# Sigmoid attention and SwiGLU in one launch: the order written out from changed planner constants, and another way of storing the last set

## The chip, the cores and the metric

The kernel runs on one core of a Trainium2 chip. The time is the device time of one execution in microseconds (us). Of the kernel before there are three timed runs, with a median of 419.71 us (419.66 to 421.11), and one profiled execution, from which every duration below is taken.

## The reference

Two blocks follow one another. The first is attention with a sigmoid in place of the softmax, on inputs of 8 batches, 12 heads, 448 rows and 64 columns:

```python
scores = scale * np.matmul(q, k.transpose(0, 1, 3, 2)) - np.log(S)
attn = 1.0 / (1.0 + np.exp(-scores))
attn_out = np.matmul(attn, v)
```

Its output, with the heads laid side by side, is x, of 3584 rows and 768 columns. The second block is a feed-forward layer of width 1536:

```python
g = x @ w_gate
silu = g * (1.0 / (1.0 + np.exp(-g)))
return (silu * (x @ w_val)) @ w_out
```

All inputs and the output are float32 in device memory.

## The kernel before

**The blocks of attention.** Four heads of a batch make a block, so a batch has 3 blocks and the whole 24, numbered i = 0 to 23. For a block the kernel loads q, k and v (448 KB each) to staging buffers, casts q and k to bf16 and v to fp16, and transposes q and k. For blocks 0 to 5 TensorE transposes (`tr_pe`, L337: seven 128x128 transposes for q and seven for k, each set copied from PSUM to the tile `qkT` by VectorE). For later blocks one transposing DMA on SyncE does both (`tr_dma`, L370). A block has 7 key slots. For each there is a burst of four score matmuls (`burst`, L381, tile `sc`) and one sigmoid on ScalarE (`sig`, L405: `pt`, 128x896, the longest kind of instruction of ScalarE here). Then 28 matmuls multiply by v (`pv`, L413), and two copies give `xT`, the transposed x that the second block reads.

**The feed-forward block.** `f1` (L455) takes a batch and one of 12 slices of 128 of the 1536 columns: six matmuls give `g`, six give `v`; ScalarE takes the sigmoid of `g` (`s`), VectorE multiplies it by `g` (`t`, which frees the PSUM slot of `g`) and then by `v` (`hT`). The tiles `g` and `v` share a ring of two PSUM slots, so the `g` of a slice waits until `t` of the slice before has read its own `g`. The gate and value weights come in four chunks (`wg_0` to `wv_3`), each loaded in three parts of 384 KB and cast by GpSimd. The last product, with w_out, is done for two blocks of 128 rows at a time (`f2_set`, L549) in a form with seven products of six matmuls instead of eight, numbered 1 to 7, whose results VectorE adds up in the output tile; sums of the weights for it are formed by VectorE (`weight_sums`, L512).

**What sets the order.** Each instruction or small group is first recorded as an operation with an engine, an assumed duration, what it depends on and which buffers it takes and gives back. A planner (`list_schedule`, L63) plays these through with its own account of time and writes all engines' instructions out in the order in which they would start; on the chip only semaphores hold. The account of a load is the line L40: one busy time per DMA from the number and size of its pieces, all loads in one chain. Two loads are lengthened by hand in the lines before `fill` (L691): the second part of k of block 0, and q of block 1. `MARGIN` (L59) is a time by which the planner lets a TensorE transpose of a block above 3 (blocks 4 and 5, L361) wait beyond the end of its cast. In the first stage, until the first `pv` of block 1, the planner also writes filler matmuls (`ps_warm`) where TensorE would idle. None of these figures is an instruction; they act through the order alone.

**The queues.** All loads, the transposing DMAs and the last stores are issued by SyncE in order. Casts of loads run on GpSimd in order, those of blocks 0 to 2 for q and k on VectorE.

**The end.** The last set (products 1 to 7 for m = 3, k = 3; tags `A` and `TO` are two PSUM rings) is stored in halves of 384 columns as soon as a half is complete (`store`, L608). A block of 128 rows there consists of two lots of 64 rows that lie at different places in the output. Before, the first lot goes out on SyncE's queue and the second on ScalarE's. The order is: half `lo` of e after `c11`, half `hi` of o after `c22`, half `hi` of e after `c12`, and half `lo` of o after `c21`, the add behind product 4 (`step7`, L668), the last of all.

Of the kernel before, what the change touches and what calls it, by code (L numbers as in the profile page):

```python
# [9 lines left out]
FP32 = mybir.dt.float32  # L10
# [17 lines left out]
class Op:  # L28
# [3 lines left out]
    def __init__(self, eng, dur, fn, deps=(), mode=("F", "F"), take=(), give=(), desc=(0, 0)):  # L32
        self.eng, self.dur, self.fn, self.mode = eng, dur, fn, mode
        self.deps = [d if isinstance(d, tuple) else (d, 0.0) for d in deps if d is not None]
        self.take = [Slot(t) for t in take]
        self.give = list(give)
        self.rank = self.t0 = self.t1 = None
        n, size = desc
        self.hold = n == 1792
        self.dma = 2.0 if n == 1792 else n / 16 * max(0.042, 0.003 + size / 24600)  # L40

    def got(self, tag):
        return [s for s in self.take if s.tag == tag]
# [12 lines left out]
NEAR = 12  # L56
VIS = 9
WO = 4
MARGIN = 0.0  # L59
FREE = set()  # L60


# [90 lines left out]
def kernel(  # L153
# [10 lines left out]
    nc = tc.nc  # L164

    B, H, S, D = q.shape
    DM = H * D
    DFF = moe_w_gate.shape[1]
    KC = DM // 128
    NF = DFF // 128  # L170
    NS = 7
# [35 lines left out]
    NH = NF // 2  # L207
# [5 lines left out]
    def wsum(j, c, n=1):  # L213

        x = (j - 1) * NH + c
        o = x % 4 * HW
        return stt[NEARLY + x // 4].bitcast(FP16)[:, o:o + n * HW]
# [6 lines left out]
    def op(*a, **kw):  # L224
        o = Op(*a, **kw)
        ops.append(o)
        return o
# [10 lines left out]
    T = {}  # L238
# [310 lines left out]
    def f2_set(m, k):  # L549


        last = k == NS // 2
        e, o = ((m - 1, NS - 1), (m, NS - 1)) if last else ((m, 2 * k), (m, 2 * k + 1))
        end = last and m == B // 2 - 1
        lo, hi = slice(0, HW), slice(HW, DM)
        P, C = {}, {}

        def blk(t, r):
            if t[0] != m:
                return kept[:, 3 * r:3 * r + 3]  # L560
            x = T["hT", m][:, r * NH:(r + 1) * NH, t[1] * 128:(t[1] + 1) * 128]
            return x.rearrange("p (a b) t -> p a b t", b=2)

        def hs(f0, f1):
            bs = {x // S for tm, t in (e, o) for x in (t * 128, t * 128 + 127) if tm == m}
            return [(R["hT", 2 * m + b, f], 0.16 * (f - f0)) for b in bs for f in range(f0, f1)] + \
                ([R["kept", m - 1, r] for r in range(2)] if last else [])

        def c(t, cols):
            return T[("osb",) + t][:, cols]  # L570

        def start(final):
            full = [d[0] if isinstance(d, tuple) else d for d in hs(0, NF)]

            def s1():
                for n in (1, 2):
                    T["s", n, m, k] = sb.tile([128, NH // 2, 2, 128], FP16, tag=f"S{n}", bufs=slots["S"],
                                              name=f"s{n}_{m}_{k}")
                nc.vector.tensor_tensor(out=T["s", 1, m, k], in0=blk(o, 0), in1=blk(o, 1), op=ADD)

            def s2():
                nc.vector.tensor_tensor(out=T["s", 2, m, k], in0=T["s", 1, m, k], in1=blk(e, 0), op=SUB)

            def s3():
                nc.vector.tensor_tensor(out=blk(o, 0), in0=blk(e, 0), in1=blk(o, 0), op=SUB)  # L585
            C["s1"] = op("DVE", 0.56, s1, deps=full, take=["S"])
            C["s2"] = op("DVE", 0.56, s2, deps=[C["s1"]])
            C["s3"] = op("DVE", 0.56, s3, deps=[C["s2"]])

        def product(n, lhs, rhs, deps, final):  # L590
            tag = "A" if final and n % 2 else "TO"

            def fn():
                if tag == "A":
                    T["p", m, k, n] = psum.tile([128, 2, 512], FP32, tag="A", bufs=2, name="ps_ol")[:, 0, 0:HW]
                else:
                    T["p", m, k, n] = psum.tile([128, HW], FP32, tag="TO", bufs=2, name="ps_o")
                for x in range(NH):
                    nc.tensor.matmul(out=T["p", m, k, n], lhsT=lhs()[:, x // 2, x % 2], rhs=rhs(x),  # L599
                                     start=x == 0, stop=x == NH - 1)  # L600
            P[n] = op("PE", 0.975, fn, deps=deps, take=[tag])

        def add(name, n, dst, other, deps, free=True):
            C[name] = op("DVE", 0.45, lambda: nc.vector.scalar_tensor_tensor(  # L604
                out=c(*dst), in0=T["p", m, k, n], scalar=HREC, in1=c(*other), op0=MULT, op1=ADD),
                deps=[P[n]] + deps, give=P[n].take if free else [])

        def store(t, deps, give, final, cols=slice(0, DM)):  # L608
            def fn(xs, dma):
                def go():  # L610
                    for x in xs:
                        bb, s = divmod(2 * t[1] + x, NS)
                        rows = slice((2 * t[0] + bb) * S, (2 * t[0] + bb + 1) * S)
                        dma.dma_start(out=out[rows, cols].rearrange("(p s) d -> s p d", s=NS)[s],  # L614
                                      in_=T[("osb",) + t][64 * x:64 * x + 64, cols])
                return go
            if end:
                op("SP", 0.5, fn([0], nc.sync), deps=deps, give=give)
                op("ACT", 0.5, fn([1], nc.scalar), deps=deps)
            else:  # L620
                op("SP" if final else "POOL", 1.1, fn([0, 1], nc.sync if final else nc.gpsimd), deps=deps, give=give)

        def step1(final):
            start(final)
            product(1, lambda: blk(e, 0), lambda x: wo16[:, x, lo],
                    hs(0, NH) + [R["wo16", f] for f in range(NF)], final)

            def fn():
                for t in (e, o):
                    if final:  # L630
                        T[("osb",) + t] = staging("osf")[:, 0:DM]
                    else:
                        T[("osb",) + t] = sb.tile([128, DM], FP32, tag="osb", bufs=slots["osb"],
                                                  name=f"osb_{t[0]}_{t[1]}")
                nc.scalar.activation(out=c(e, lo), in_=T["p", m, k, 1], func=COPY, scale=HREC)
            C["p1"] = op("ACT", 0.45, fn, deps=[P[1]], take=["osf" if final else "osb"] * 2, give=P[1].take)

        def step2(final):
            w = [R["ws", 4, x] for x in range(0, NH, 2)]
            product(6, lambda: T["s", 2, m, k], lambda x: wsum(2, x), [C["s2"]] + w, final)  # L640
            add("u2", 6, (e, hi), (e, lo), [C["p1"]])

        def step3(final):
            product(2, lambda: blk(e, 1), lambda x: wo16[:, NH + x, lo], hs(NH, NF), final)
            C["s4"] = op("DVE", 0.56, lambda: nc.vector.tensor_tensor(
                out=blk(e, 1), in0=blk(e, 1), in1=T["s", 2, m, k], op=SUB), deps=[P[2], C["s2"]])
            add("c11", 2, (e, lo), (e, lo), [C["u2"]])
            if end:
                store(e, [C["c11"]], [], final, lo)

        def step4(final):
            product(7, lambda: blk(o, 0), lambda x: wsum(3, x), [C["s3"]], final)
            add("u3", 7, (o, lo), (e, hi), [C["u2"]])

        def step5(final):
            product(5, lambda: T["s", 1, m, k], lambda x: wsum(1, x), [C["s1"]], final)
            add("u4", 5, (e, hi), (e, hi), [C["u3"]], free=False)
            add("c22", 5, (o, hi), (o, lo), [C["u3"]])
            P[5].give = C["s1"].take
            if end:  # L660
                store(o, [C["c22"]], [], final, hi)

        def step6(final):
            product(3, lambda: blk(e, 1), lambda x: wo16[:, NH + x, hi], [C["s4"]], final)
            add("c12", 3, (e, hi), (e, hi), [C["u4"]])
            store(e, [C["c11"], C["c12"]], C["p1"].take[:1], final, hi if end else slice(0, DM))

        def step7(final):  # L668
            product(4, lambda: blk(o, 1), lambda x: wsum(4, x), hs(NH, NF), final)
            add("c21", 4, (o, lo), (o, lo), [C["u3"], C["c22"]])  # L670
            store(o, [C["c21"], C["c22"]], C["p1"].take[1:], final, lo if end else slice(0, DM))
            R.setdefault(("f2", m), []).extend(P.values())
        return [(0.5, x) for x in (step1, step2, step3, step4, step5, step6, step7)]


# [10 lines left out]
    op("ACT", 1.5, lambda: nc.scalar.activation(out=warm, in_=sb_t, func=SIGM))  # L686
    loads(1, "qk")
    R["st_k", 0][1].dma += 1.0
    R["st_q", 1][0].dma += 0.4
    loads(0, "v")  # L690
    def fill(n):  # L691

# [151 lines left out]
```

## Time and profile before

| What | us |
|---|---|
| median of three runs | 419.71 |
| profiled execution: its own time | 420.82 |
| profiled execution: span from first to last instruction | 419.03 |
| TensorE busy | 410.4 (98%) |
| VectorE, ScalarE, GpSimd busy | 237.7, 217.5, 133.3 |
| mean granted TensorE clock | 0.999 of full |

In the profile PE is TensorE, PEld its weight loads, DVE VectorE, ACT ScalarE, POOL GpSimd and SP SyncE; a q behind a name is an engine's DMA-issuing sequencer. A timeline row gives the start in us, the busy time, the engine and the line, output tile and input, the number of merged instructions, and in brackets how long the engine had been idle before and what released it. A matmul's end is modelled and overlaps with the next one, so distances between starts are the better measure on PE. "To landing" is the time from the issue of a DMA to its completion. The time of an execution lies between 0.7 (the median) and 1.8 us (its own time) above the span; the span is what is worked with below.

### The profile page before, as it was taken

The page shows a single profiled execution, that of the slowest core. Times are in us where ns is not written, and L with a number is a line of the kernel's source. Part 1 is how long each engine was busy: PE and PEld are TensorE (multiplying, and loading weights), DVE is VectorE, ACT ScalarE, POOL GpSimd, SP SyncE. Part 2 cuts the span into 40 slices and gives each one's busy share as a digit, 9 for nine tenths or more (in the row PEclk, how much of TensorE's full clock was granted, in tenths as well). Part 3 has the DMA queues.
Part 4 walks back from the last instruction along what each step waited for, and adds up shares of the span by engine and source line. Part 5 has one row for each costly group of instructions (what it writes and reads, how often), then busy time and mean ns, then how long its engine had stood idle before and what let it go on. Part 6 is the DMA issues. An engine that isn't in the chain of part 4 may idle for free.

```text
span 419.0 us, 7945 instructions
## 1 busy us (share of the span) xinstructions
PE 410.4 (98%) x3194; PEld 205.1 (49%) x3194; DVE 237.7 (57%) x420; ACT 217.5 (52%) x290; POOL 133.3 (32%) x196
## 2 busy tenths in 40 slices
PE   8989999999999999999999999999999999999995
PEld 3434444444445554544454554554545545555563
DVE  3544544467667644564574745647556465565873
ACT  5986778778751165467445565455455552122000
POOL 1788865764360232424031431403400100000000
PEclk9999999999999999999999999999999999999999
DMA  8999999997980284488067373482500302020235
GB/s 266 380 375 377 375 286 340 314 314 184 229 248 2 76 215 83 150 172 236 2 177 125 127 223 74 140 144 100 120 2 0 77 2 75 2 74 1 60 95 150
DMA packets 64693, 66.97 MB, mean 160 GB/s; under 512 B 35536, under 2 KB 60880, under 8 KB 64656
## 3 DMA queue, kind: packets, MB, share of 16 engines
q1 hardware_dynamic: 62704, 59.39, 49.7%
q0 software_dynamic: 1632, 6.69, 6.3%
q8 instruction: 25, 0.41, 0.4%
q10 hardware_dynamic: 320, 0.39, 0.3%
q14 instruction: 12, 0.10, 0.1%
HBM read 47.19 MB, written 11.01 MB: 139 GB/s over the span
## 4 chain that ended last, share of the span: by engine, by line
PE 90%; DMA 6%; DVE 1%; ACT 1%; SPq 0%; issue 0%; POOL 0%; POOLq 0%
PE ps_g L466 26%; PE ps_v L466 23%; PE ps_o L599 18%; PE ps_sc L391 8%; PE ps_pv L426 7%; PE ps_ol L599 5%; DMA st<-in_k_dram 4%; PE ps_vl L466 3%; DMA st<-in_v_dram 3%; ACT pt L408 0%; SPq L265 0%; PE ps_tr L348 0%; DVE t L476 0%; DVE hT L585 0%; POOL src L235 0%
## 5 line engine op out<-in xcount | busy, mean ns | idle before, releaser
L408 ACT ACTIVATE pt<-ps_sc,sbiast 128x896 f16<-128x896 f32 x168 | 159.0, 1007 | 28.8 <-PE ps_sc L391 28.8
L466 PE MATMUL ps_g<-xT,wg 128*128 128x448 f16 x576 | 124.0, 353 | 0.5 <-DVE t L476 0.5
L472 ACT ACTIVATE s<-ps_g 128x448 f16<-128x448 f32 x96 | 52.2, 544 | 123.5 <-PE ps_g L466 122.7
L476 DVE TENSOR_TENSOR t<-ps_g,s 128x448 f16<-128x448 f32 x96 | 59.9, 624 | 92.3 <-ACT s L472 92.2
L466 PE MATMUL ps_v<-xT,wv 128*128 128x448 f16 x504 | 109.9, 353 | 0.0
L466 PEld LDWEIGHTS <-wg 128*128 128x128 f16 x576 | 54.9, 98 | 54.8 <-issue 6.7
L466 PEld LDWEIGHTS <-wv 128*128 128x128 f16 x576 | 52.0, 98 | 59.1 <-issue 17.6
L235 POOL CAST src<-st 128x896 bf16<-128x896 f32 (+1 forms) x43 | 40.3, 937 | 96.8 <-DMA st<-in_q_dram 66.7
L482 DVE SCALAR_TENSOR_TENSOR hT<-ps_v,t 128x448 f16<-128x448 f32 x84 | 52.4, 624 | 32.0 <-PE ps_v L466 31.1
L391 PE MATMUL ps_sc<-qkT 64*64 64x448 bf16 x672 | 50.8, 360 | 0.8 <-ACT pt L408 0.6
L599 PEld LDWEIGHTS <-hT 128*128 128x128 f16 x384 | 37.6, 98 | 27.2
L235 POOL CAST v<-st 64x448 f16<-64x448 f32 (+1 forms) x72 | 42.2, 586 | 22.4 <-DMA st<-in_v_dram 8.7
L614 POOL DMA_DIRECT2D out_dram<-osb x34 | 17.7, 525 | 93.6 <-DVE osb L604 93.5
L426 PE MATMUL ps_pv<-pt,v 64*64 64x448 f16 x672 | 37.7, 351 | 0.2
L604 DVE SCALAR_TENSOR_TENSOR osb<-ps_o,osb 128x384 f32<-128x384 f32 x63 | 34.0, 551 | 6.2 <-PE ps_o L599 6.2
L233 DVE CAST xT<-ps_pv 128x448 f16<-128x448 f32 x40 | 23.4, 619 | 20.7 <-PE ps_pv L426 20.7
L599 PE MATMUL ps_o<-wo,hT 128*128 128x384 f16 x168 | 31.9, 326 | 0.0
L391 PEld LDWEIGHTS <-qkT 64*64 64x64 bf16 x672 | 14.8, 105 | 29.0 <-issue 25.2
L426 PEld LDWEIGHTS <-v 64*64 64x64 f16 x672 | 19.3, 107 | 14.6 <-issue 3.8
L599 PE MATMUL ps_o<-st,s 128*128 128x384 f16 x138 | 26.2, 326 | 0.0
L599 PE MATMUL ps_o<-st,hT 128*128 128x384 f16 x138 | 26.2, 326 | 0.0
L599 PEld LDWEIGHTS <-s 128*128 128x128 f16 x168 | 16.4, 98 | 11.8
(44 smaller groups left out, 195.6 us busy)
## 6 DMA issues: line engine op xcount, KB each, us to landing
st<-in_q_dram SPq DMA_DIRECT2D x24, 448.0 KB, 5.3
st<-in_v_dram SPq DMA_DIRECT2D x24, 448.0 KB, 6.3
st<-in_k_dram SPq DMA_DIRECT2D x23, 448.0 KB, 5.5
out_dram<-osb POOLq DMA_DIRECT2D x34, 192.0 KB, 3.1
st<-in_moe_w_gate_dram SPq DMA_DIRECT2D x12, 384.0 KB, 8.8
st<-in_moe_w_val_dram SPq DMA_DIRECT2D x12, 384.0 KB, 8.8
st<-in_moe_w_out_dram SPq DMA_DIRECT2D x12, 384.0 KB, 6.9
out_dram<-st SPq DMA_DIRECT2D x16, 192.0 KB, 2.7
```

The source lines that it names most:

```text
L233: nc.vector.tensor_copy(out=o, in_=i)
L235: nc.gpsimd.tensor_copy(out=o, in_=i)
L391: nc.tensor.matmul(out=sc[64 * (g ^ a):64 * (g ^ a) + 64, a, 0:S].rearrange("k (s p) -> k s p", s=NS), lhsT=kT[r, s, 64 * g:64 * g + 64], ...
L408: nc.scalar.activation(out=pt, in_=T[("sc",) + key][:, :, 0:S], func=SIGM, bias=sb_t, scale=qkscale)
L426: nc.tensor.matmul(out=T["pv", i, a][64 * g:64 * g + 64, :], lhsT=T["v16", i][r, a, s, :], rhs=T["pt", i, s][r, a, :], start=(s == 0), sto ...
L466: nc.tensor.matmul(out=T[nm, b, f], lhsT=w[c][:, j, ff * 128:(ff + 1) * 128], rhs=T["xT", b, j], start=(j == 0), stop=(j == KC - 1))
L472: nc.scalar.activation(out=t, in_=T["g", b, f], func=SIGM)
L476: nc.vector.tensor_tensor(out=t, in0=T["g", b, f], in1=T["s16", b, f], op=MULT)
L482: nc.vector.scalar_tensor_tensor(out=T["hT", m][:, f, o * S:(o + 1) * S], in0=T["v", b, f], scalar=HSC, in1=T["t1", b, f], op0=MULT, op1=MULT)
L599: nc.tensor.matmul(out=T["p", m, k, n], lhsT=lhs()[:, x // 2, x % 2], rhs=rhs(x), start=x == 0, stop=x == NH - 1)
L604: C[name] = op("DVE", 0.45, lambda: nc.vector.scalar_tensor_tensor(out=c(*dst), in0=T["p", m, k, n], scalar=HREC, in1=c(*other), op0=MULT, ...
L614: dma.dma_start(out=out[rows, cols].rearrange("(p s) d -> s p d", s=NS)[s], in_=T[("osb",) + t][64 * x:64 * x + 64, cols])
```

## The change

Four constants of the account change: a load of 1792-byte pieces is taken to last a little longer, `MARGIN` goes from 0 to 1 us, and the hand-made addition to q of block 1 from 0.4 to 1.0. The last set's halves are stored with one DMA for all 128 rows where the two lots can be addressed together (they can in all four halves here), and each whole half goes to one queue: SyncE's, but ScalarE's for `c22` and for the first part of `c21`. Product 4 of the last set is split by columns into two products of six 192-column matmuls, each with its own add and store.

```diff
-        self.dma = 2.0 if n == 1792 else n / 16 * max(0.042, 0.003 + size / 24600)
+        self.dma = 2.0 if n == 1792 else n / 16 * max(0.042, size / 22300 - 0.003)
-MARGIN = 0.0
+MARGIN = 1.0
         def product(n, lhs, rhs, deps, final):
-            tag = "A" if final and n % 2 else "TO"
+            tag = "A" if final and n in (1, 3, 5, 7) else "TO"
+            w = HW if n in range(8) else HW // 2
...
-            P[n] = op("PE", 0.975, fn, deps=deps, take=[tag])
+            P[n] = op("PE", 0.975 * w / HW, fn, deps=deps, take=[tag])
...
-        def store(t, deps, give, final, cols=slice(0, DM)):
-            def fn(xs, dma):
+        def store(t, deps, give, final, cols=slice(0, DM), eng="SP"):
+            def fn(dma):
                 def go():
-                    for x in xs:
+                    for x in (0, 1):
                         bb, s = divmod(2 * t[1] + x, NS)
                         rows = slice((2 * t[0] + bb) * S, (2 * t[0] + bb + 1) * S)
-                        dma.dma_start(out=out[rows, cols].rearrange("(p s) d -> s p d", s=NS)[s],
-                                      in_=T[("osb",) + t][64 * x:64 * x + 64, cols])
+                        dst = out[rows, cols].rearrange("(p s) d -> s p d", s=NS)
+                        src = T[("osb",) + t][:, cols]
+                        if end and x == 0 and s + 1 < NS:
+                            dma.dma_start(out=dst[s:s + 2], in_=src)
+                            break
+                        dma.dma_start(out=dst[s], in_=src[64 * x:64 * x + 64])
                 return go
             if end:
-                op("SP", 0.5, fn([0], nc.sync), deps=deps, give=give)
-                op("ACT", 0.5, fn([1], nc.scalar), deps=deps)
+                op(eng, 0.5, fn(nc.sync if eng == "SP" else nc.scalar), deps=deps, give=give)
...
             if end:
-                store(o, [C["c22"]], [], final, hi)
+                store(o, [C["c22"]], [], final, hi, "ACT")
...
-            product(4, lambda: blk(o, 1), lambda x: wsum(4, x), hs(NH, NF), final)
-            add("c21", 4, (o, lo), (o, lo), [C["u3"], C["c22"]])
-            store(o, [C["c21"], C["c22"]], C["p1"].take[1:], final, lo if end else slice(0, DM))
+            for n, cols in ((4.1, slice(0, HW // 2)), (4.2, slice(HW // 2, HW))) if end else ((4, lo),):
+                product(n, lambda: blk(o, 1), lambda x, cols=cols: wsum(4, x)[:, cols], hs(NH, NF), final)
+                add("c21", n, (o, cols), (o, cols), [C["u3"], C["c22"]])
+                store(o, [C["c21"], C["c22"]], C["p1"].take[1:] if n != 4.1 else [], final, cols if end else slice(0, DM),
+                      "ACT" if n == 4.1 else "SP")
...
-    R["st_q", 1][0].dma += 0.4
+    R["st_q", 1][0].dma += 1.0
```

The instructions as they are then written out differ from those before in these places only: on TensorE within the first 80 groups (up to the third slice of the feed-forward block) and in the last product; on VectorE where two transposed tiles of block 4 are copied, where the weight sums are formed (between 92 and 110 us in the profile before), and in the last add; on ScalarE by one sigmoid that goes ahead of one copy of `xT`, and in the last stores; on SyncE in the last stores. GpSimd's order and the order of all loads stay the same.

More of the change, by code (lines that the diff above doesn't have):

```diff
@@ L590, in product @@
         def product(n, lhs, rhs, deps, final):
-            tag = "A" if final and n % 2 else "TO"
+            tag = "A" if final and n in (1, 3, 5, 7) else "TO"
+            w = HW if n in range(8) else HW // 2
             def fn():
                 if tag == "A":
-                    T["p", m, k, n] = psum.tile([128, 2, 512], FP32, tag="A", bufs=2, name="ps_ol")[:, 0, 0:HW]
+                    T["p", m, k, n] = psum.tile([128, 2, 512], FP32, tag="A", bufs=2, name="ps_ol")[:, 0, 0:w]
                 else:
-                    T["p", m, k, n] = psum.tile([128, HW], FP32, tag="TO", bufs=2, name="ps_o")
+                    T["p", m, k, n] = psum.tile([128, w], FP32, tag="TO", bufs=2, name="ps_o")
                 for x in range(NH):
@@ L600, in fn @@
                                      start=x == 0, stop=x == NH - 1)
-            P[n] = op("PE", 0.975, fn, deps=deps, take=[tag])
+            P[n] = op("PE", 0.975 * w / HW, fn, deps=deps, take=[tag])
         def add(name, n, dst, other, deps, free=True):
-            C[name] = op("DVE", 0.45, lambda: nc.vector.scalar_tensor_tensor(
+            C[name] = op("DVE", 0.45 if n in range(8) else 0.28, lambda: nc.vector.scalar_tensor_tensor(
                 out=c(*dst), in0=T["p", m, k, n], scalar=HREC, in1=c(*other), op0=MULT, op1=ADD),
                 deps=[P[n]] + deps, give=P[n].take if free else [])
-        def store(t, deps, give, final, cols=slice(0, DM)):
-            def fn(xs, dma):
+        def store(t, deps, give, final, cols=slice(0, DM), eng="SP"):
+            def fn(dma):
                 def go():
-                    for x in xs:
+                    for x in (0, 1):
                         bb, s = divmod(2 * t[1] + x, NS)
                         rows = slice((2 * t[0] + bb) * S, (2 * t[0] + bb + 1) * S)
-                        dma.dma_start(out=out[rows, cols].rearrange("(p s) d -> s p d", s=NS)[s],
-                                      in_=T[("osb",) + t][64 * x:64 * x + 64, cols])
+                        dst = out[rows, cols].rearrange("(p s) d -> s p d", s=NS)
[4 more added lines that the diff above has]
+                        dma.dma_start(out=dst[s], in_=src[64 * x:64 * x + 64])
                 return go
             if end:
-                op("SP", 0.5, fn([0], nc.sync), deps=deps, give=give)
-                op("ACT", 0.5, fn([1], nc.scalar), deps=deps)
+                op(eng, 0.5, fn(nc.sync if eng == "SP" else nc.scalar), deps=deps, give=give)
             else:
-                op("SP" if final else "POOL", 1.1, fn([0, 1], nc.sync if final else nc.gpsimd), deps=deps, give=give)
+                op("SP" if final else "POOL", 1.1, fn(nc.sync if final else nc.gpsimd), deps=deps, give=give)
         def step1(final):
```

## The prediction

> **What bounds the kernel now.** I read the page's busy times and slices first:
>
> ```profile
> PE 410.4 (98%) x3194; PEld 205.1 (49%) x3194; DVE 237.7 (57%) x420; ACT 217.5 (52%) x290; POOL 133.3 (32%) x196
> PE   8989999999999999999999999999999999999995
> DMA  8999999997980284488067373482500302020235
> ```
>
> TensorE is the bound nearly throughout; the DMA engines are full besides for the first nine slices (94 us). PE's timeline from 31.1 us to its last product shows only two idle times, 0.30 us at 66.22 and 0.24 us at 119.99. So a change of order can gain only in the first 31 us and behind the last product; whatever TensorE gains before 31 us reaches the end, unless an input that comes by DMA is not there yet.
>
> TensorE's timeline at the start of the feed-forward block:
>
> ```profile
> 28.28 0.54 PE L466 MATMUL ps_v<-xT,wv 128*128 128x448 f16 x2
> 29.50 0.56 PE L348 MATMUL ps_tr<-idn,src 128*128 128x128 bf16 x7 [0.68 <-POOL src L235]
> 29.90 0.54 PE L466 MATMUL ps_v<-xT,wv 128*128 128x448 f16 x2
> 30.70 0.56 PE L348 MATMUL ps_tr<-idn,src 128*128 128x128 bf16 x7 [0.26 <-POOL src L235]
> ```
>
> Both transposes of block 4 stand in PE's queue ahead of work that could run; their casts wait for loads. This is 0.68 + 0.26 = 0.94 us. The next product (g of the second slice) starts at 31.10. ScalarE's timeline, then VectorE's, before that:
>
> ```profile
> 10.52 6.39 ACT L408 ACTIVATE pt<-ps_sc,sbiast 128x896 f16<-128x896 f32 x7 [0.50 <-PE ps_sc L391]
> 17.50 9.25 ACT L408 ACTIVATE pt<-ps_sc,sbiast 128x896 f16<-128x896 f32 x10 [0.60 <-PE ps_sc L391]
> 27.26 0.53 ACT L231 CAST xT<-ps_pv 128x448 f16<-128x448 f32 x1 [0.51 <-PE ps_pv L426]
> 27.69 1.01 ACT L408 ACTIVATE pt<-ps_sc,sbiast 128x896 f16<-128x896 f32 x1
> ...
> 29.17 0.62 DVE L476 TENSOR_TENSOR t<-ps_g,s 128x448 f16<-128x448 f32 x1 [1.32 <-ACT s L472]
> ```
>
> From 6.3 to 26.75 us ScalarE is the bound: 21 sigmoids at 0.925 us (9.25 / 10), with only two holes, 0.50 and 0.60 us, where the next burst stood in PE's queue behind a transpose: that of q of block 1, whose cast ended at 9.53, and that of q of block 2, which waited for a PSUM slot until 16.45.
>
> The end, from the timeline of VectorE and TensorE:
>
> ```profile
> 412.88 1.53 DVE L604 SCALAR_TENSOR_TENSOR st<-ps_ol,st 128x384 f32<-128x384 f32 x3 [0.39 <-PE ps_ol L599]
> 413.66 1.14 PE L599 MATMUL ps_o<-st,hT 128*128 128x384 f16 x6
> 414.83 0.56 DVE L604 SCALAR_TENSOR_TENSOR st<-ps_o,st 128x384 f32<-128x384 f32 x1 [0.42 <-PE ps_o L599]
> ```
>
> The last add ends at 415.39; the two halves of its store are issued at 415.4 and land after 2.3 (SyncE) and 2.5 us (ScalarE), at 417.7 and 417.9. The span ends 1.1 us later.
>
> [...] the page shows 98 ns. But weight loads overlap with matmuls: 14 transposes of 128 columns with a load each take 0.79 us (two sets of 0.40, from the starts 29.50, 29.90, 30.70, 31.10), 56 ns a pair. So 192-column matmuls should not be held up by their loads. [...] the last matmul is over at 414.8, the granted clock is 1.00 until 418.0 and 0.50 after. Nothing here idles so long earlier. [...] the halves of a store land 0.2 us apart. [...]
>
> **Part 1, q of block 1 later in the account (with the load figures).** One burst now stands ahead of the transpose of q of block 1, and so one more ahead of that of block 2. The first hole closes: the PSUM slot of that burst is free at 9.09 (6.31 + 3 x 0.925), the sigmoid can follow at 10.01. The second hole closes too: twelve instead of eleven bursts stand ahead of the transpose at 16.5. The transposes themselves are not later, as they wait for the cast and the slot. I followed each burst of the new order up to block 2's last (slot free, then burst, then sigmoid) and found each in time. ScalarE gains 0.50 + about 0.53: the 21st sigmoid ends near 25.72 instead of 26.75. Fillers change by one or two at a time (0.2 us each) and stand only where TensorE waits anyway; if that cover were gone they would cost those 0.2 us. Below, the loss is at worst the whole gain.
>
> **Part 2, MARGIN.** The two transposes (0.40 us each) now follow g and bursts of the second and third slice; the 0.94 us of waiting leave the queue. What is late next is the ring of two PSUM slots: g of the second slice waits for t of the first. Before, t ended 2.10 us after the sigmoid at 27.69 began (29.79). After: the 21st sigmoid ends at 25.72, + 0.24 (burst after sigmoid, 26.99 - 26.75) + 0.38 (two g matmuls now in between) = 26.34 for the burst, + 0.41 (a burst's start to its sigmoid's, 41.18 to 41.59) = 26.75, say 26.8, for its sigmoid, + 2.10 + 0.05 = 28.95 for g of the second slice. TensorE itself would be there at about 28.5, so it idles some 0.5 us. Before, that g began at 31.10 with 0.80 us of transposes done that now come later: gain 31.10 - 28.95 - 0.80 = 1.35.
>
> With MARGIN alone the sigmoid stays at 27.69, g could start at 29.84, and the gain would be 0.46; with part 1 alone the transposes still wait for the loads, which PE's order doesn't move, and the gain is about nothing.
>
> **What cuts it.** Three inputs come by DMA and are not earlier:
>
> ```profile
> 37.13 0.83 POOL L306 CAST wv<-st 128x768 f16<-128x768 f32 x1 [0.23 <-DMA st<-in_moe_w_val_dram]
> 50.41 5.36 SPq L374 DMA_TRANSPOSE qkT<-src x1
> DMA to landing us min/median/max: 7.9/7.9/7.9
> 59.40 0.57 PE L391 MATMUL ps_sc<-qkT 64*64 64x448 bf16 x8
> ```
>
> The last part of wv_1 is cast by 37.96; the fifth matmul of its first product stood at 38.59 + 0.76 = 39.35, so 1.39 us may be gained there. wv_0's last part (cast over at 28.05) is wanted at about 28.0. The first transposing DMA (block 6) lands at 50.41 + 7.9 = 58.31, + 0.14 for the wait (29.57 to 29.71 for a load and its cast): 58.45. The second half of the burst at 59.40 reads it, at 59.59: 1.14 us may be gained. This is the tightest. Head: 1.1 us, bounds 0.3 and 1.3. Block 4's transposed k is due at the burst of 38.09, then about 37.0; it is copied behind t of the third slice, by about 35.8: covered by 1.2 us. The later transposes move no DMA, since GpSimd and SyncE keep their order, and the source buffer that they free is wanted for block 6's cast only at 48.25. The reordered weight sums (VectorE, 92 to 102 us) and the sigmoid ahead of a copy of xT there have no PE wait in view: nothing, or 0.2 us either way.
>
> **Part 3, the end.** Product 4 in two: twelve matmuls of 192 columns, half of 162 ns each (413.66 less 412.68 is 0.98 for six): 0.98 again; bound above 12 x 98 ns = 1.18. The first add may run when VectorE is free at 414.41 and ends at about 414.77; the second starts at 414.83 as the whole one did and takes 0.345 (0.624 at 448 columns, 0.555 at 384, so 1.08 ns a column) instead of 0.56: over at 415.17, 0.21 earlier. The last set issues five DMAs instead of eight; the new waits stand on ScalarE and SyncE, behind which only the next store is queued, and ScalarE has no other work then. The last store is one DMA of 96 KB alone; before, 192 KB went out then. The 16 engines move 184 to 286 GB/s in the windows of 0.5 us from 415.0 to 417.5, so 96 KB less is 0.35 us. Landing: 415.19 + 2.1 to 2.2 (the shortest that the 96 KB stores show) = 417.35 against 417.93: 0.6 us, bounds 0 (one queue with twice the pieces loses what two gained) and 0.8.
>
> **Sum.** 1.1 + 0.6 = 1.7: span 419.03 - 1.7 = 417.3. The median lies 0.68 above the span (the profiled execution's own time 1.8 above): 418.0. A measurement of this kernel can tell about 0.5% from no change, which is 2.1 us: 417.6 and 421.8 are the borders.
>
> **Rivals.** A, the forecast: 1.4 to 2.05 us gained, 0.54. B, the loads decide anyway: a DMA in the full stretch lands a little later, or the ring of g and v binds harder, so that 0.5 of the head is left: 418.6; for it speaks that three inputs have under 0.3 us to spare, against it that none grows. 0.20. C, the whole-block stores are no faster (one ring carries twice the pieces, 768 bytes each): the tail gives 0 to 0.2, total 1.2: 418.5. 0.08. D, more than 2.1 gained: the bounds 1.3 + 0.8, or one of the holes at 66 and 120 us closing: 417.3. 0.12. E, slower: block 4's transposed k. Its copy is behind t on VectorE, which is behind two sigmoids on ScalarE. Every us past the burst at 37.0 stalls TensorE by one; the copy would have to end after 37.0 + 1.7 = 38.7, 2.9 us later than worked out, before the kernel is slower, and 5 later for 0.5%: 422. The trace has no such delay in the same chain at block 5. With causes of this kind unseen: 0.06.
>
> **The numbers.** 418.0 is A's. Low 417.1 is D's bound with a little spread of runs; high 419.7 covers B, C and no gain. Faster by over 0.5%: D and a small part of A, 0.16; slower: 0.06; the rest 0.78.
>
> **What would show it.** The holes of 0.5 and 0.6 us gone from ScalarE; the 21st sigmoid over by 25.8; no PE wait on GpSimd's cast at 29 to 31 but about 0.5 us on t; the burst of blocks 5 and 6 at 58.3, with a short wait on the DMA; the last matmul at 413.7; the last landing 2.5 us after it. Wrong if a wait of PE over 0.5 us appears after 31 us, or if the last store lands over 2.4 us after its issue.

## The result, and the profile after

| | before | changed |
|---|---|---|
| median, us | 419.69 (418.94 to 421.11, 6 runs) | 433.62 (433.04 to 434.80, 6 runs) |
| ratio, 95% interval | | 1.0331 (1.0310 to 1.0352) |
| profiled execution: own time, span | 420.82, 419.0 | 433.43, 431.6 |
| mean granted TensorE clock | 0.999 | 0.984 |

The changed kernel is 13.9 us slower, where 1.7 us less was forecast. Nothing of it lies in the arithmetic: TensorE is busy for 409.8 us, 0.6 less than before. The page of the changed kernel, busy times and slices:

```profile
PE 409.8 (95%) x3198; PEld 205.5 (48%) x3200; DVE 238.2 (55%) x421; ACT 217.5 (50%) x290; POOL 133.4 (31%) x196
PE   8999999999999999999999999999999999999940
PEclk9999999999999999999999999999999999999985
DMA  8999999997650667393637536645003020202321
```

The last one and a half slices (of 10.8 us each) hold no work of TensorE, its granted clock is 0.50 there from 418 us on (which is all of the lower mean clock), and the DMA engines are busy by one to two tenths.

The head went as the prediction had it. ScalarE's timeline and then TensorE's, changed kernel:

```profile
6.14 19.32 ACT L408 ACTIVATE pt<-ps_sc,sbiast 128x896 f16<-128x896 f32 x21 [0.53 <-PE ps_sc L391]
26.94 1.01 ACT L408 ACTIVATE pt<-ps_sc,sbiast 128x896 f16<-128x896 f32 x1 [0.30 <-PE ps_sc L391]
```

```profile
29.09 1.30 PE L466 MATMUL ps_g<-xT,wg 128*128 128x448 f16 x6 [0.46 <-DVE t L476]
30.31 0.57 PE L391 MATMUL ps_sc<-qkT 64*64 64x448 bf16 x8
30.82 0.56 PE L348 MATMUL ps_tr<-idn,src 128*128 128x128 bf16 x7
```

The 21 sigmoids are one row now, so both holes are closed; the transposes of block 4 come behind g and find their casts done; g of the second slice starts at 29.09 (28.95 forecast) after a wait of 0.46 us on t (0.5 forecast). This is one execution against one; the section on the head sets it beside others.

The end, from the timeline of the changed kernel (q behind a name is the issuing sequencer):

```profile
413.29 1.15 PE L600 MATMUL ps_o<-st,hT 128*128 128x192 f16 x12
413.57 1.76 ACTq L618 DMA_DIRECT2D out_dram<-st  x2
413.99 0.85 DVE L605 SCALAR_TENSOR_TENSOR st<-ps_o,st 128x192 f32<-128x192 f32 x2
414.08 1.30 SPq L618 DMA_DIRECT2D out_dram<-st  x2
```

The last add is over at 413.99 + 0.85 = 414.84, 1.55 us after its product starts; before it was 415.39 - 413.66 = 1.73. That gain of 0.18 is the forecast 0.21. Both queues have issued everything by 415.4. But the span goes on to 431.6. What happens there is in the windows (columns: stretch, its length, busy time of PE, PEld, DVE, ACT, POOL, then the granted clock, the busy share of the 16 DMA engines and their GB/s). First the kernel before:

```profile
415.00:415.50 0.50, 0.00 (x0) 0.00 (x0) 0.39 (x1) 0.00 (x0) 0.00 (x0) 1.00 0.88 184
415.50:416.00 0.50, 0.00 (x0) 0.00 (x0) 0.00 (x0) 0.00 (x0) 0.00 (x0) 1.00 0.91 286
416.00:416.50 0.50, 0.00 (x0) 0.00 (x0) 0.00 (x0) 0.00 (x0) 0.00 (x0) 1.00 0.96 283
```

Then the changed kernel:

```profile
414.00:416.00 2.00, 0.45 (x6) 0.22 (x3) 0.70 (x3) 0.00 (x0) 0.00 (x0) 1.00 0.13 28
418.00:420.00 2.00, 0.00 (x0) 0.00 (x0) 0.00 (x0) 0.00 (x0) 0.00 (x0) 0.50 0.13 51
420.00:422.00 2.00, 0.00 (x0) 0.00 (x0) 0.00 (x0) 0.00 (x0) 0.00 (x0) 0.50 0.13 50
426.00:430.00 4.00, 0.00 (x0) 0.00 (x0) 0.00 (x0) 0.00 (x0) 0.00 (x0) 0.50 0.14 46
```

A share of 0.13 that stays so for 16 us is what two engines of sixteen give that are never idle (2/16 = 0.125), at 25 GB/s each from 416 us on; the view has the mean share, and the two are worked out from it. 4 x 192 KB at 50 GB/s take 15.7 us. The whole-block store addresses the output as [2, 64, 384]: two lots, 64 rows, 384 columns; the store of one lot addresses [64, 384].

The lots of 64 rows reach a share of 0.96 in the windows before. The prediction took the share of the 16 engines for granted and never asked how the new pattern would be divided among them.

### The profile page after: what moved, and what is told of

Read it like the earlier page. It is cut to its first block, busy times and chain, and to the rows that moved or that the text cites. A ratio compares the mean times of both kernels' runs of the same rounds, so it can differ in the third digit from the quotient of the medians.

```text
span 431.6 us, 7948 instructions
## 1 busy us (share of the span) xinstructions
PE 409.8 (95%) x3198; PEld 205.5 (48%) x3200; DVE 238.2 (55%) x421; ACT 217.5 (50%) x290; POOL 133.4 (31%) x196
## 4 chain that ended last, share of the span: by engine, by line
PE 81%; DMA 6%; ACT 4%; DVE 2%; POOL 1%; SPq 1%; issue 1%; POOLq 0%; DVEq 0%; ACTq 0%
PE ps_g L466 23%; PE ps_v L466 19%; PE ps_o L600 18%; PE ps_sc L391 7%; PE ps_pv L426 6%; PE ps_ol L600 5%; DMA st<-in_v_dram 4%; ACT pt L408 4%; PE ps_vl L466 3%; DMA st<-in_q_dram 1%; POOL v L235 1%; SPq L265 1%; PE ps_tr L348 1%; DVE st L523 0%; DVE t L476 0%
## 5 line engine op out<-in xcount | busy, mean ns | idle before, releaser
L482 DVE SCALAR_TENSOR_TENSOR hT<-ps_v,t 128x448 f16<-128x448 f32 x84 | 52.3, 623 | 31.7 <-PE ps_v L466 30.8
L600 PE MATMUL ps_o<-wo,hT 128*128 128x384 f16 x168 | 31.9, 326 | 0.0
L391 PEld LDWEIGHTS <-qkT 64*64 64x64 bf16 x672 | 14.8, 105 | 30.2 <-issue 25.7
L600 PE MATMUL ps_o<-st,hT 128*128 128x384 f16 (+1 forms) x144 | 26.2, 320 | 0.0
```

The source lines that it names most:

```text
L391: nc.tensor.matmul(out=sc[64 * (g ^ a):64 * (g ^ a) + 64, a, 0:S].rearrange("k (s p) -> k s p", s=NS), lhsT=kT[r, s, 64 * g:64 * g + 64], ...
L482: nc.vector.scalar_tensor_tensor(out=T["hT", m][:, f, o * S:(o + 1) * S], in0=T["v", b, f], scalar=HSC, in1=T["t1", b, f], op0=MULT, op1=MULT)
```

## The experiments

**The whole-block store, undone and alone.** In the changed kernel, three lines out and each queue keeping its halves:

```diff
-                        if end and x == 0 and s + 1 < NS:
-                            dma.dma_start(out=dst[s:s + 2], in_=src)
-                            break
```

> The changed kernel with only the whole-block form undone: each half of the last set goes out in two DMAs of 64 rows on the queue that the change gives it; the order, the split product and the queues stay. Theory W (a store whose output pattern has 2 as its outermost count runs on two DMA engines only): all of the loss is gone, 1.4 to 1.9 us faster than before, 0.995 to 0.997. Rival Q (the loss is from the queue or the split product): still some 433 us. Rival O (the new order costs time later on): above before.

Measured: 420.98 us (10 runs), ratio 1.0034 (1.0022 to 1.0045). Of the loss 12.6 us are gone, but the forecast gain of the rest is not there.

In the kernel before, all four halves as whole blocks on SyncE's queue, order and products as before:

```diff
+                    if end:
...
+                        dma.dma_start(out=out[rows, cols].rearrange("(p s) d -> s p d", s=NS)[s:s + 2],
+                                      in_=T[("osb",) + t][:, cols])
+                        return
...
-                op("ACT", 0.5, fn([1], nc.scalar), deps=deps)
```

> The kernel before with only the last set's four halves stored in whole blocks, all on SyncE's queue; order and product 4 as before. W: 4 x 192 KB at the 50 GB/s of the changed kernel's tail is 15.7 us from about 413, so the last landing at about 429.5 to 430.5 instead of 417.9 and 432 to 434 us, ratio 1.028 to 1.036. Rivals Q and O: within 1 us of before.

Measured: 432.13 us (4 runs), ratio 1.0296 (1.0282 to 1.0309). This one part is 12.4 of the 13.9 us.

**Is it the number of rows, or the form of the store?** The kernel before with each lot of the last set as two plain two-dimensional stores, of 62 and 2 rows, and in a control of 48 and 16:

```diff
-                        dma.dma_start(out=out[rows, cols].rearrange("(p s) d -> s p d", s=NS)[s],
-                                      in_=T[("osb",) + t][64 * x:64 * x + 64, cols])
+                        for r0, r1 in ((0, 62), (62, 64)) if end else ((0, 64),):
+                            dma.dma_start(out=out[rows, cols].rearrange("(p s) d -> s p d", s=NS)[s][r0:r1],
+                                          in_=T[("osb",) + t][64 * x + r0:64 * x + r1, cols])
```

> The kernel before, each lot of 64 rows of the last set stored as 62 rows and 2 rows, two-dimensional, on the queues of before. Theory K ([...]62 rows run on 2 engines and not on 16, just as the whole block with its outermost count of 2 does): 744 of the 768 KB pass over two engines at about 50 GB/s, 15 us, and the time is 1.024 to 1.032 of before. Rival F (it is the three-dimensional form of the whole-block store, or its 128 partitions, that is slow): eight more issues at 0.5 to 0.8 us over two queues, 1.001 to 1.007.

> Control to e8_rows62: each lot as 48 and 16 rows, so also two stores where one was[...]. Theory K: all 16 engines carry every store; what is left is the cost of twice as many issues on each queue, 0.6 to 2.5 us: ratio 1.001 to 1.006. Rival F: the same, and no difference from e8_rows62.

Measured: 62 + 2 rows 431.67 us (2 runs), ratio 1.0271 (1.0240 to 1.0302); 48 + 16 rows 420.43 us (20 runs), 1.0010 (1.0000 to 1.0019). The windows at 62 + 2 rows, then at 48 + 16:

```profile
418.00:420.00 2.00, 0.00 (x0) 0.00 (x0) 0.00 (x0) 0.00 (x0) 0.00 (x0) 0.50 0.13 51
422.00:426.00 4.00, 0.00 (x0) 0.00 (x0) 0.00 (x0) 0.00 (x0) 0.00 (x0) 0.50 0.13 50
```

```profile
415.00:416.00 1.00, 0.00 (x0) 0.00 (x0) 0.00 (x0) 0.00 (x0) 0.00 (x0) 1.00 0.73 200
416.00:417.00 1.00, 0.00 (x0) 0.00 (x0) 0.00 (x0) 0.00 (x0) 0.00 (x0) 0.60 0.69 198
```

Both have twice as many stores and the same bytes. 62 rows run with the same share and rate as the whole block (0.13, 50 GB/s), two engines' worth. 48 and 16 rows reach a share of 0.73, which takes about twelve engines or more (0.73 x 16 = 11.7). So K holds where it was tried, and F falls: cutting the 64 rows at 62 instead of at 48 makes 11.2 us. What sets the number of engines for other counts was not shown. Half of these bytes were issued on each queue, and from 418 to 427 us each queue has a share of 0.065, together 0.13, not twice that; in the changed kernel it is 0.067 and 0.066 from 418 to 425 us. The narrow stores of both queues shared two engines' worth. What the issues cost is seen in the control: 0.4 us for eight more.

**One half alone.** The kernel before with only the last half (`lo` of o), or only the first (`lo` of e), as a whole block:

```diff
+            whole = end and (t == o and cols == lo)
...
+                    if whole:
...
+                        dma.dma_start(out=out[rows, cols].rearrange("(p s) d -> s p d", s=NS)[s:s + 2],
+                                      in_=T[("osb",) + t][:, cols])
+                        return
...
```

> The kernel before with the last of the four halves alone stored as a whole block. Theory K: its 192 KB leave over two engines in 3.9 us at 50 GB/s, where the last two lots took part in a stream of 200 to 280 GB/s: 2.2 to 3.2 us later, ratio 1.005 to 1.008. Rival F, that a whole-block store is slow by a fixed amount each (the 12.4 us of e2_whole_only over four stores): 3.1 us, so this run separates little, and e9_first_whole does.

> The kernel before with the first of the four halves alone stored as a whole block, some 3.5 us before the last add ends. Theory K: its 96 KB on each of two engines stand there in front of these engines' shares of the six later lots (36 KB each): 132 KB at about 25 GB/s is 5.3 us from about 412.8 us on, to 418.1 us instead of 417.4 us: 0.3 to 1.0 us slower, ratio 1.0005 to 1.0025. A fixed amount for each whole-block store would be 3.1 us, ratio 1.0074; a store that is only slow itself and holds up nothing behind it would cost nothing, 0.999 to 1.0005.

Measured: last half 423.29 us (4 runs), ratio 1.0071 (1.0053 to 1.0089); first half 422.00 us (6 runs), 1.0041 (1.0026 to 1.0055). The last half costs what K gave for it. The first half, issued 3.3 us before the last add ends, is not hidden, and costs 1.7 us (1.1 to 2.3); the fixed amount (3.1) and the harmless store (0) are both excluded, and K's own 0.3 to 1.0 was too low. The first half alone, windows:

```profile
414.00:415.00 1.00, 0.39 (x3) 0.01 (x1) 0.57 (x2) 0.00 (x0) 0.00 (x0) 1.00 0.16 37
415.00:416.00 1.00, 0.00 (x0) 0.00 (x0) 0.00 (x0) 0.00 (x0) 0.00 (x0) 1.00 0.44 69
417.00:418.00 1.00, 0.00 (x0) 0.00 (x0) 0.00 (x0) 0.00 (x0) 0.00 (x0) 1.00 0.88 303
418.00:419.00 1.00, 0.00 (x0) 0.00 (x0) 0.00 (x0) 0.00 (x0) 0.00 (x0) 1.00 0.17 60
```

From 418.2 to 419.2 the share is again that of two engines (0.13 to 0.14, 49 GB/s), which fits K: they finish alone what stood behind the whole block. But the six later lots lift the share above 0.24 only from about 415.2 on, and slowly at first (0.32, then 0.71 and 0.64 in quarters of a us), although these are issued from 413.5 on (in the kernel before from 413.9, and the engines are at a share of 0.88 from 415.0). The later lots, on both queues, land later. Size and median time to landing of the lots in the kernel before, then of the six with the first half whole:

```profile
out_dram<-st SPq DMA_DIRECT2D x4, 96.0 KB, 2.2
out_dram<-st ACTq DMA_DIRECT2D x4, 96.0 KB, 2.5
```

```profile
out_dram<-st SPq DMA_DIRECT2D x3, 96.0 KB, 5.1
out_dram<-st ACTq DMA_DIRECT2D x3, 96.0 KB, 4.9
```

Why the share rises so late is open; K doesn't say it, and it is what K's figure lacks.

**The head alone.** The kernel before with the four planner constants:

```diff
-        self.dma = 2.0 if n == 1792 else n / 16 * max(0.042, 0.003 + size / 24600)
+        self.dma = 2.0 if n == 1792 else n / 16 * max(0.042, size / 22300 - 0.003)
-MARGIN = 0.0
+MARGIN = 1.0
...
-    R["st_q", 1][0].dma += 0.4
+    R["st_q", 1][0].dma += 1.0
```

> The kernel before with only the four constants of the planner changed (the order of the changed kernel; end as before). The prediction's head: 1.1 us faster, as the profile of the changed kernel shows 1.24 us at the fourth slice's g; ratio 0.997 to 0.9975. Rival O: not faster, or slower.

Measured: 420.35 us (15 runs), ratio 1.0013 (1.0002 to 1.0024). The gain of 1.1 us is not there; it is rather 0.5 us dearer.

The runs leave one profiled execution each, and executions differ by what lands when at the start. One point of the work can be followed through all of them: the products `hT` on VectorE (L482), 96 in each. Starts in us:

| profiled execution | order of the head | 19th hT | 19th to 21st | 19th to 96th | 96th to the end |
|---|---|---|---|---|---|
| before | before | 92.10 | 7.27 | 295.44 | 31.5 |
| all whole blocks | before | 90.82 | 7.27 | 295.70 | 44.0 |
| split alone | before | 90.46 | 7.27 | 295.30 | 31.8 |
| split, third queue | before | 90.78 | 7.27 | 295.39 | 32.5 |
| 62 + 2 rows | before | 90.66 | 7.43 | 295.79 | 44.1 |
| 48 + 16 rows | before | 91.27 | 7.35 | 295.65 | 31.9 |
| first half | before | 91.53 | 7.35 | 295.60 | 33.7 |
| last half | before | 90.23 | 7.32 | 295.62 | 35.3 |
| sums later, head as before | before | 91.57 | 7.27 | 295.38 | 31.5 |
| changed kernel | new | 90.86 | 8.69 | 296.31 | 44.4 |
| changed, in lots | new | 92.28 | 7.83 | 295.66 | 31.9 |
| head alone | new | 91.17 | 8.66 | 296.28 | 31.5 |
| changed, two queues | new | 90.85 | 8.24 | 296.29 | 31.8 |
| head, sums later | new | 92.38 | 7.27 | 295.42 | 31.4 |

The 19th hT shows two things. The execution from which I predicted is the latest of nine with the order of before (median 90.82); the changed kernel's 90.86 is 1.24 us better than that one and no better than the median. In the other eight of the old order the two holes of the sigmoids together are mostly 0.2 to 0.4 us instead of 1.1 (0.9 in one), and in five of them the transposes of block 4 don't wait at all, because their casts, which wait for loads, were done: there was little to gain. The new order does close the holes in all its five executions, but in all five g of the second slice also waits 0.46 us on t, where it doesn't in any of the old order. So the new order is not ahead there: its 19th hT lies between 90.85 and 92.38, with a median of 91.17 (two of the five had a late load, of which more below). And the next columns show a loss that only the new order has, at 92 to 99 us: from the 19th to the 96th hT it takes 296.3 us in three executions, where the median of the old order is 295.6. (In the changed kernel in lots it takes 295.66; TensorE came there 1.4 us later.)

VectorE's timeline there, split alone (order of before):

```profile
89.29 0.62 DVE L476 TENSOR_TENSOR t<-ps_g,s 128x448 f16<-128x448 f32 x1 [1.08 <-ACT s L472]
...
91.00 0.78 DVE L523 TENSOR_TENSOR st<-wo 128x768 f16<-128x768 f16 x1
91.86 1.00 DVE L523 TENSOR_TENSOR st<-wo,st 128x768 f16<-128x768 f16 x1
92.79 0.61 DVE L476 TENSOR_TENSOR t<-ps_g,s 128x448 f16<-128x448 f32 x1
...
96.92 0.61 DVE L476 TENSOR_TENSOR t<-ps_g,s 128x448 f16<-128x448 f32 x1
```

and in the changed kernel:

```profile
92.57 0.62 DVE L476 TENSOR_TENSOR t<-ps_g,s 128x448 f16<-128x448 f32 x1 [1.08 <-ACT s L472]
93.11 1.64 DVE L523 TENSOR_TENSOR st<-wo 128x768 f16<-128x768 f16 x2
94.68 0.55 DVE L523 TENSOR_TENSOR st<-wo,st 128x768 f16<-128x768 f16 x1
95.15 0.61 DVE L233 CAST xT<-ps_pv 128x448 f16<-128x448 f32 x1
95.68 0.61 DVE L482 SCALAR_TENSOR_TENSOR hT<-ps_v,t 128x448 f16<-128x448 f32 x1
96.21 0.54 DVE L523 TENSOR_TENSOR st<-wo 128x768 f16<-128x768 f16 x1
96.68 1.75 DVE L523 TENSOR_TENSOR st<-wo,st 128x768 f16<-128x768 f16 x2
98.35 0.61 DVE L476 TENSOR_TENSOR t<-ps_g,s 128x448 f16<-128x448 f32 x1
```

Each t has to be over before TensorE may write the g after it. In the order of before, two weight sums go ahead of the t at 92.79, in time that VectorE has free after the hT that ends at 91.1. In the new order the whole burst stands behind that t: six sums, a copy and an hT fill VectorE without a gap from 93.1 until the next t at 98.35, and TensorE shows the price (changed kernel):

```profile
99.01 1.29 PE L466 MATMUL ps_g<-xT,wg 128*128 128x448 f16 x6 [0.92 <-DVE t L476]
```

To test it, the head alone with the weight sums asked for later, and the same in the kernel before as a control:

```diff
-            if i > WO + 4 or i == WO + 4 and sl > 1:
+            if i > WO + 5:
                 for _ in range(WSN):
                     next(wsums, None)
```

> The head's new order alone (e3_head_only) with the twelve weight sums on VectorE (L523) asked for some slices later, so that they are spread over about 95 to 116 us instead of standing in one burst at 93 to 99 us. Theory Q (in e3_head_only the TensorE lead of about 0.9 us that the head gains is eaten at 99 us, because t of the next gate product stands on VectorE behind that burst, whose start hangs on the casts of wo): the 0.88 us wait of the gate product on t at 99.3 us is gone, and the time falls by 0.4 to 0.9 us against e3_head_only: ratio to before 0.9990 to 1.0004. Rival R (the new order is dear for another reason, such as transposes that wait in other blocks): the wait at 99 us goes or shrinks, but the time stays at the 1.0013 of e3_head_only or above.

> The kernel before with the weight sums alone spread in the same way, the head's order as before. Theory Q: before has no wait of the gate product on t at 99 us, so there is nothing to gain but the 0.24 us wait at 120 us: ratio 0.9990 to 1.0005. If the spread itself costs or brings something (the second products start later, since they ask for the sums), this run shows it and e11_sums_later must be read against it rather than against e3_head_only. Rival R gives no difference between this run and before either, but then e11_sums_later lies 0.5 us or more above this run.

Measured: head with sums later 420.11 us (14 runs), ratio 1.0005 (0.9995 to 1.0016); control 419.81 us (14 runs), 0.9988 (0.9976 to 1.0000). In the trace of the head with the sums spread, the stretch from the 19th to the 21st hT takes 7.27 us, and g starts without a wait. But the changed kernel in lots, whose burst of sums isn't spread, has no wait there either. The head with sums later, then the changed kernel in lots:

```profile
99.45 1.30 PE L466 MATMUL ps_g<-xT,wg 128*128 128x448 f16 x6
```

```profile
99.43 1.29 PE L466 MATMUL ps_g<-xT,wg 128*128 128x448 f16 x6
```

Both executions are late at the 19th hT (92.38 and 92.28), and so late the wait is gone with the burst as it was. The trace therefore doesn't show that it was the spreading that removed it. Nor do the times: 1.0005 lies just above what Q gave, and the intervals of the two head kernels overlap. The control came out lower than it was expected, and the head with the sums spread is dearer than it by 0.3 us in the medians and by 0.7 in the ratios; rival R's mark was 0.5. So the burst costs TensorE 0.7 to 0.9 us at this place where it arrives early, but Q as the cause of the head's time is not shown, and R is not excluded.

In the profiled executions of these two kernels the second part of k of block 0 landed late: its cast began at 7.9 us, in most others at 6.1 to 6.7, and TensorE waited 1.3 to 1.4 us for it; it happened once in nine with the old order too (48 + 16 rows, a wait of 0.5). The loads stand in the same order in all of them. Which of the planner's constants moves the sums was not run apart.

**The split product.** The changed kernel's order and split, with each lot on its queue as before; the split alone in the order of before; and the split with its first quarter from GpSimd's queue:

```diff
...
-                op(eng, 0.5, fn(nc.sync if eng == "SP" else nc.scalar), deps=deps, give=give)
+                op("SP", 0.5, fn(nc.sync, [0]), deps=deps, give=give)
+                op("ACT", 0.5, fn(nc.scalar, [1]), deps=deps)
```

```diff
+                if eng == "POOL":
+                    op("POOL", 1.1, fn(nc.gpsimd), deps=deps, give=give)
+                else:
...
-                      "ACT" if n == 4.1 else "SP")
+                      "POOL" if n == 4.1 else "SP")
```

> New order, product 4 in two parts, but every half in two lots of 64 rows, one on SyncE's and one on ScalarE's queue as before. The prediction's head and tail without the whole blocks: 1.4 to 1.8 us faster than before; against the run with each half on one queue within 0.3 us[...].

> The kernel before with the last product and its add in two parts alone, each part's lots of 64 rows on the two queues as before (five stores on each queue instead of four); head and planner figures as before. Theory S (the last add ends 0.5 us earlier, but issuing is serial on each sequencer at 0.5 to 0.8 us a store, so the fifth store is issued no earlier than the fourth was): ratio 1.000 to 1.0025. Rival T (the 0.9 us between e7_two_queues and e3_head_only came from elsewhere, and the split gains what the prediction had for the earlier add, 0.2 to 0.5 us): ratio 0.9985 to 0.9995.

> As e14_split_only, but the first quarter of the split product is stored from GpSimd's queue, both lots, so that SyncE and ScalarE issue four stores each as before and the last quarter's are issued as soon as its add has ended. Theory S: 0.4 to 0.8 us less than e14_split_only, at 0.9985 to 1.0005 of before, with the last stores issued about 0.1 us after the last add. Rival T: no difference from e14_split_only. A store from GpSimd that is issued or lands later (a median of 3.1 us from issue to landing for its 192 KB pairs in before) would make it slower than e14_split_only.

Measured: new order and split on two queues 421.21 us (6 runs), ratio 1.0040 (1.0024 to 1.0056); split alone 420.32 us (14 runs), 1.0011 (1.0001 to 1.0021); split with a third queue 421.50 us (6 runs), 1.0036 (1.0022 to 1.0050). The first, with everything of the change but the whole-block store and its choice of queues, was to be 1.4 to 1.8 us faster and is slower than either of its parts (head alone 1.0013, split alone 1.0011); their sum is at the lower end of its interval. Against the run with each half on one queue (420.98) it is 0.2 us, as was expected. The split gains nothing, and T falls. The timeline of the kernel before, then of the split alone:

```profile
413.93 1.95 SPq L614 DMA_DIRECT2D out_dram<-st  x3
413.94 2.03 ACTq L614 DMA_DIRECT2D out_dram<-st  x3
```

```profile
412.58 0.85 DVE L605 SCALAR_TENSOR_TENSOR st<-ps_o,st 128x192 f32<-128x192 f32 x2
412.72 1.85 SPq L617 DMA_DIRECT2D out_dram<-st  x3
412.76 2.12 ACTq L617 DMA_DIRECT2D out_dram<-st  x3
```

Before, the queues have issued their last store 0.49 and 0.58 us after the last add (415.88 and 415.97 against 415.39). With the split, it is 1.14 and 1.45 us after it (414.57 and 414.88 against 413.43): stores of 0.6 to 0.7 us each stand in a row, and the last quarter waits behind the first. This is what S described. But the remedy that S proposed made it slower: with the first quarter on GpSimd's queue the last bytes pass at about 416.2, 30.0 us after the 96th hT (30.2 with the split alone, 29.9 before), and then the span runs on for 2.5 us to 418.7, where it is 1.6 us in the other two. So in this execution the program with a store on GpSimd's queue ended 0.9 us later after its last bytes; what it waits for there, the trace doesn't show.

## Why the prediction was wrong

**Part 3, the end: the step that failed.** The working was "96 KB less is 0.35 us" at the rate of 184 to 286 GB/s that the windows showed for lots of 64 rows, with a bound of 0 below. That rate was carried over to stores of another pattern, which ran at 28 to 51 GB/s. So the term that was put at 0.6 us gained measured 44.4 - 31.5 = 12.9 us of loss, of which the whole-block store alone is 12.4 (e2_whole_only) and the split about 0.4. Rival C named the whole-block store and priced it by pieces and queues, not by engines, so its worst was no gain; nothing in the range had a cost at this place. Both signs of being wrong that were written down came true: a last landing over 2.4 us after its issue (the last one was issued by 415.4, and the engines moved bytes until 430.2), and a wait of TensorE over 0.5 us after 31 us (0.92 at 99.01).

**The last add** 0.21 us earlier: measured 0.18. Right, but the split alone is not faster, as its issues stood in a row ("behind which only the next store is queued" was true, and that store was the last one). The 98 ns of the prediction is the page's mean for one weight load; the twelve matmuls with their loads took 1.15 us, the six before 1.14.

**Part 1 and Part 2, the head.** The mechanisms came as described: holes gone (the 21st sigmoid over at 25.46, forecast 25.72), 0.94 us of waits on casts gone, 0.46 us on t instead (0.5), the second g at 29.09 (28.95), the head 1.24 us better than the profiled execution before (1.1). What failed is that one execution stood for the kernel. The text saw that it was 1.1 us slower than the median, and booked the difference as the distance from the span to the time: "the median lies 0.68 above the span". In each of the runs the own time is 1.8 us above its own span; the profiled execution was simply late by 1 us, and most of the waits that were booked as gain are not there in most executions of the same order, while the 0.46 us on t stand in all five of the new one.

**"The reordered weight sums have no PE wait in view: nothing, or 0.2 us either way."** The second step that failed: measured 0.92, 0.88 and 0.67 us of waiting in three of the four executions with the burst. The bound was taken from the old order, in which t has room, instead of following t through VectorE's new queue.

**What cuts it.** The transposing DMA of block 6 did not bind: the burst that reads it starts at 58.16, without a wait. Of rival B the loads did not come true, but the ring of g and v did bind harder, by those 0.67 to 0.92 us on t; B expected half of the head's gain to be left, and none was. E's late copy did not occur.

Together, the changed kernel's profiled execution against the medians of the old order: head 0 (90.86 against 90.82), from the 19th to the 96th hT 0.7 (296.3 against 295.6), tail 12.9, sum 13.6 us; the medians of the times differ by 13.9. Only the tail is shown by runs that leave it out and that have it alone. That the 0.7 us are the burst of sums is read from traces, and the run that spread it didn't confirm it.

**Better than both.** None of the runs is measurably faster than the kernel before; the lowest is the control with the sums spread, 0.9988 (0.9976 to 1.0000).

## What to carry to other kernels

When a change joins or cuts DMAs, write down the outermost count of both access patterns before pricing anything: a store of two lots as [2, 64, ...] ran at the share of two engines of sixteen (0.13) and took about five times as long per byte as two stores of [64, ...] (50 GB/s against 184 to 286), and 62 rows did the same. One store for the two halves of the 128 partitions, whose other side has the halves apart as an outer dimension of 2, was dearer here than two stores: 12.4 us in four. Before a wait in a profile is booked as gain, ask whether it belongs to the kernel or to that one execution: here an own time 1.1 us above the median pointed to the latter.

## What the runs showed that was not expected

- A narrow store that is issued early is not hidden behind 3.3 us of other work: 192 KB at two engines' worth (a share of 0.13 to 0.16 from 413 to 415 us), issued first, cost 1.7 us at the end, as the later stores on both queues landed after 4.9 to 5.1 us instead of 2.2 to 2.5.
- The same order of loads lands differently from one execution to the next: the 19th hT of the old order lies between 90.23 and 92.10 us.
- Cutting each of the last eight stores in two (48 + 16 rows) cost 0.4 us in all; cutting the last two alone, in the split, cost as much; there the trace shows the added ones in a row after the last add.
- With one pair of stores on GpSimd's queue at the end of the program, the time from the last byte to the end was 2.5 us instead of 1.6, in one profiled execution each.
